# Talking-heads attention with a gated feed-forward on one core: score blocks of 112 rows, two blocks' score products ahead of the first mix, one pool of four PSUM banks

## The chip, the cores and the metric

The kernel runs on one core of a Trainium2 chip. The metric is the device time of one execution in microseconds (us), as the median of several runs. The profile and the trace come from one execution of their own.

## The reference

Attention whose heads are mixed before and after the softmax, then a feed-forward with a gated activation. Batch B = 4, H = 12 heads, S = 448 rows, D = 64; the feed-forward has 768 inputs and 2048 hidden units.

```python
scores = scale * np.matmul(q, k.transpose(0, 1, 3, 2))
scores = np.einsum('bhij,hg->bgij', scores, w_pre)
scores = scores - np.max(scores, axis=-1, keepdims=True)
attn = np.exp(scores)
attn = attn / (np.sum(attn, axis=-1, keepdims=True) + 1e-09)
attn = np.einsum('bhij,hg->bgij', attn, w_post)
x = np.matmul(attn, v)          # then (B, H, S, D) -> (B * S, H * D)
...
h = x @ w_in
g = h * (1.0 / (1.0 + np.exp(-1.702 * h)))
return (g @ w_out).astype(np.float32)
```

## The kernel before

**Scores.** The rows of a batch are cut into four blocks of 120, 120, 120 and 88 rows (`chunk`, `CI`, `NCH`). For each block `b, c` and each of six pairs of heads, `scores` makes two products q k^T of 448 columns, one per head, in two PSUM banks (tiles `qk`, lines 247 and 257). ScalarE (ACT) and VectorE (DVE) copy them to a tile `sc` in SBUF (lines 269 to 279), and `send_scores` (line 283) writes it to a DRAM tensor `sd`, one for each block. Batches 0 and 1 (`b < WHOLE`) work in fp32; batches 2 and 3 carry an upper and a lower fp16 part.

**Steps.** The head mix needs all 12 heads of a row on the partitions. So a step `i` takes 10 rows (`GI`): `gather` (lines 295, 300) reads 120 partitions (10 rows by 12 heads) of 448 values from `sd` into a tile `r`, of which there are four (`AHEAD`), and `mix` multiplies it by a block matrix of `w_pre` into `mx`. A batch has 45 steps (`GPB`, the last with 8 rows), the kernel 180 (`N`). `peak` (DVE) takes the maximum, `expo` (ACT) the exponential and its sum, `shifted` (POOL) and `inverse` (DVE) the reciprocal, `weigh_mix` (POOL) scales the `w_post` matrix to `wr`, and `post_whole` multiplies, with the head mix after the softmax in it, into `pp`; ACT copies that to `p`. In fp16 the names are `weigh`, `upper`, `lower` and `post`. Twelve steps fill one block of `p` (120 rows); `context` then multiplies six pairs of heads by v into `av`, three pairs at a time, and the results become columns of `x`.

**Feed-forward.** A unit is one of 8 slices of the hidden units of one batch: `hidden` (`h`, line 604) and `project` (`po`, line 642), in sessions of 6 matmuls or more. The weights arrive as 64-bit numbers. 16 conversions read them (`w`, three loads of 512 KB each), turn them into fp16 pairs on ACT and DVE and store them in DRAM (`wd`); each unit then loads its two slices (`wt`, 768 KB each). The feed-forward of a batch can start when its last `context` is done.

**PSUM** has eight banks: three of tag `gen` for `qk`, `h` and `po`, one of tag `av`, two for `mx`, two for `pp`.

**What sets the order.** All instructions go out in an order that a planner fixes when the program is built. `add` enters a task with an engine, a planned duration, the tasks it comes after, the buffers it takes and a due time; `run_all` (line 752) picks for each engine the earliest due among the tasks that could start, and books a model of the DMA (`DMA["rate"]`, `lanes` for eight transfers under way). It adds 0.1 us on PE where products of scores or context (`PART`) meet another kind, but doesn't order by it. A task of kind `late` isn't started while more than 1.5 us of transfers are booked; nothing has that kind. All transfers are issued by one queue, SP's, in the planned order.

**The head** is written out by hand (lines 822 to 894): six loads of q and k, 10 products of a matrix of ones, then block 0's six pairs in `gen`, `mx` and `pp` banks by turns, each pair's first 48 rows sent at once (`FRONT`), the four first gathers, the other 72 rows of each pair, and 16 more products of ones (`idle_products(16)`). The planner takes over from there; block 1's pairs come due one by one from step 0 on (`x = pr`), each in a tile of tag `sc`, of which there are three.

## Time and profile before

| | us |
|---|---|
| median of 3 runs | 910.88 (909.64 to 911.83) |
| the profiled execution's own time | 909.49 |
| its span, first to last instruction | 907.8 |
| PE matmul busy in it | 878.1 (97%) |
| DVE, ACT, POOL busy | 633.6, 630.5, 342.8 |

The profiled execution is 1.7 us longer than its span and 1.4 us (0.15%) below the median of the runs. PE is the engine with the least to spare, so the table is read by asking where PE stands idle or is slowed, and who ends that. DMA share is the mean busy share of the core's 16 DMA engines.

### The profile page before, as it was taken

To read this page: it belongs to the slowest core of one execution; us is meant where nothing else is said; L and a number is where in the kernel's file an instruction comes from. 1 tells how busy PE (TensorE), PEld (TensorE's weight loads), DVE (VectorE), ACT (ScalarE), POOL (GpSimd) and SP (SyncE) were. 2 spreads that over 40 slices of the span, in tenths; PEclk is the share of its full clock that TensorE was granted. 3 is DMA by queue.
4 is the path that set the end of the run, shared out by engine and by line. 5 is a ranking of instruction groups with operands and counts; after the bars stand their busy time and mean duration, and the time that the engine had idled before them with its cause. 6 is when DMAs were issued, how large, how long until landed. Compare 5 with 4: busy or idle time off the path is not lost.

```text
span 907.8 us, 19395 instructions
## 1 busy us (share of the span) xinstructions
PE 878.1 (97%) x7062; PEld 538.5 (59%) x7062; DVE 633.6 (70%) x1471; ACT 630.5 (69%) x1391; POOL 342.8 (38%) x538
## 2 busy tenths in 40 slices
PE   7889999999999999999999999999999999999998
PEld 5465666666566566655666656665656666545554
DVE  3668887678789988999678876679676664342233
ACT  2778888698877877876788797676776765323442
POOL 0212222222124221566346745547254663203332
PEclk9989999999999999999999999999999999999999
DMA  7878999998997796688587486568553432243422
GB/s 237 277 285 290 304 326 319 323 308 268 336 331 251 238 300 198 219 234 311 169 265 251 147 258 175 175 180 243 163 154 127 152 97 91 109 139 121 139 74 92
DMA packets 66402, 196.85 MB, mean 217 GB/s; under 512 B 7714, under 2 KB 32546, under 8 KB 66306
## 3 DMA queue, kind: packets, MB, share of 16 engines
q1 hardware_dynamic: 66306, 195.62, 66.7%
q8 instruction: 55, 0.90, 0.4%
q14 instruction: 41, 0.34, 0.1%
HBM read 138.96 MB, written 56.62 MB: 215 GB/s over the span
## 4 chain that ended last, share of the span: by engine, by line
PE 66%; DVE 13%; DMA 7%; ACT 7%; POOL 3%; issue 2%; SPq 1%; ACTq 0%; POOLq 0%; DVEq 0%
PE h L604 19%; PE po L642 18%; PE mx L312 5%; PE pp L363 5%; PE qk L247 3%; PE av L441 3%; PE av L452 3%; DMA vb<-in_v_dram 2%; PE qk L257 2%; DMA sd<-sc 2%; DVE nm L322 2%; DMA r<-sd 2%; PE mx L315 2%; PE pp L400 1%; PE pp L402 1%
## 5 line engine op out<-in xcount | busy, mean ns | idle before, releaser
L604 PE MATMUL h<-x,wt 128*128 128x448 f16 x1152 | 246.5, 352 | 2.0 <-DVE sc L273 0.9
L642 PE MATMUL po<-g,wt 128*128 128x448 f16 x1152 | 239.0, 352 | 2.4 <-DVE th L623 2.1
L604 PEld LDWEIGHTS <-wt 128*128 128x128 f16 x1152 | 108.9, 98 | 105.6 <-issue 15.6
L642 PEld LDWEIGHTS <-wt 128*128 128x128 f16 x1152 | 110.2, 98 | 101.5 <-issue 8.0
L343 POOL TENSOR_SCALAR rs<-sm 120x1 f32<-120x1 f32 x180 | 45.2, 251 | 319.0 <-ACT e L332 311.0
L322 DVE TENSOR_REDUCE nm<-mx 120x1 f32<-120x448 f32 x180 | 111.0, 617 | 36.4 <-PE mx L317 17.9
L670 POOL TENSOR_TENSOR acc<-acc,pt 128x448 f32<-128x448 f32 x69 | 78.7, 1141 | 114.0 <-ACT pt L664 113.3
L363 PEld LDWEIGHTS pp<-wr,e 120*112 120x112 f32 x720 | 85.1, 177 | 37.5 <-issue 18.7
L387 POOL TENSOR_TENSOR a<-w,a 120x448 f16<-120x448 f32 (+1 forms) x90 | 96.0, 1066 | 22.7 <-POOL w L373 11.2
L623 DVE SCALAR_TENSOR_TENSOR th<-th,h 128x448 f32<-128x448 f32 x64 | 39.5, 618 | 92.4 <-ACT th L619 92.1
L363 PE MATMUL pp<-wr,e 120*112 120x120 f32 x720 | 90.9, 270 | 3.9 <-POOL wr L353 3.7
L312 PE MATMUL mx<-r,wa 120*120 120x448 f32 x180 | 87.1, 569 | 5.8 <-DMA r<-sd 4.4
L332 ACT ACTIVATE e<-mx,nm,c 120x448 f32<-120x448 f32 (+1 forms) x90 | 65.3, 725 | 33.2 <-DVE nm L324 23.3
L373 POOL TENSOR_SCALAR w<-e,rs 120x448 f32<-120x448 f32 (+1 forms) x90 | 64.9, 721 | 42.7 <-DVE rs L348 25.1
L666 DVE SCALAR_TENSOR_TENSOR acc<-po,ct,acc 128x448 f32<-128x448 f32 x99 | 66.8, 677 | 15.9 <-PE po L642 15.3
L332 ACT ACTIVATE e<-mx,nm 120x448 f32<-120x448 f32 (+1 forms) x90 | 56.8, 632 | 28.5 <-DVE nm L322 24.9
L664 ACT ACTIVATE pt<-po,ct 128x448 f32<-128x448 f32 x69 | 43.6, 633 | 46.6 <-PE po L642 46.6
L381 ACT ACTIVATE a<-e,rs 120x448 f16<-120x448 f32 (+1 forms) x90 | 59.8, 668 | 20.2 <-DVE rs L348 17.4
L427 DVE TENSOR_TENSOR p<-pp,p 112x480 f16<-112x480 f32 (+1 forms) x90 | 58.3, 649 | 10.8 <-ACT p L423 10.1
L619 ACT ACTIVATE th<-h,ct 128x448 f32<-128x448 f32 x64 | 40.3, 630 | 36.0 <-PE h L604 36.0
L273 DVE SCALAR_TENSOR_TENSOR sc<-qk,sc 120x448 f16<-120x448 f32 (+1 forms) x96 | 55.5, 615 | 10.5 <-ACT sc L269 9.7
L423 ACT CAST p<-pp 112x480 f16<-112x480 f32 (+1 forms) x90 | 50.2, 557 | 17.8 <-PE pp L402 17.6
(141 smaller groups left out, 1604.7 us busy)
## 6 DMA issues: line engine op xcount, KB each, us to landing
...
```

The source lines that it names most:

```text
L312: nc.tensor.matmul(mx[:K, :S], st["wa"][:K, :K], r[:K, :], start=True, stop=True)
L322: nc.vector.tensor_reduce(nm[:K], row["mx", i][:K, :S], axis=AX.X, op=ALU.max, negate=True)
L332: nc.scalar.activation(e[:K], row.pop(("mx", i))[:K, :S], AF.Exp, bias=row.pop(("nm", i))[:K, 0:1], scale=1.0 if b < WHOLE else st["c", b] ...
L363: nc.tensor.matmul(pp[:CP, jc * K:(jc + 1) * K], e[:K, jc * CP:(jc + 1) * CP], wr[:K, :, :n], start=True, stop=True,)
L373: nc.gpsimd.tensor_scalar(w[:K], e[:K], row["rs", i][:K, 0:1], 1.0, op0=ALU.mult, op1=ALU.mult)
L381: nc.scalar.activation(a1[:K], row["e", i][:K], AF.Copy, scale=row["rs", i][:K, 0:1])
L387: nc.gpsimd.tensor_tensor(a2[:K], row.pop(("w", i))[:K], row["a1", i][:K], op=ALU.subtract)
L427: nc.vector.tensor_tensor(p[:, 1], row.pop(("pp", i)), p[:, 0], op=ALU.subtract)
L604: nc.tensor.matmul(h, w[:, i, c, fc * 128:(fc + 1) * 128], x[:, j, c, :], start=(n == 0), stop=(n == len(terms) - 1),)
L642: nc.tensor.matmul(po, w[:, j, fc, e * 128:(e + 1) * 128], g[:, i, fc, :], start=(n == 0), stop=(n == len(terms) - 1),)
L666: nc.vector.scalar_tensor_tensor(a, po, c, a, op0=ALU.mult, op1=ALU.add)
L670: nc.gpsimd.tensor_tensor(a, a, st.pop(("pt", u, e)), op=ALU.add)
```

## The change

The scores are cut into four blocks of 112 rows (`QI`, `block`); steps keep their 10 rows and `p` its 120. So three steps in each batch lie across two blocks and gather in two transfers (`blocks_of`): 12 more gathers in all. In the head the first 64 rows are sent first, not 48, and the 16 products of ones after it are gone. Blocks 1 and 2 of batch 0 (`NEAR`) get tiles of tags that the feed-forward uses later, their products are due at once, and their sends, like the loads of v and of the weights, become `late`, so that gathers go ahead of them. `gen` has four banks, and `context` and the products of ones use it too; tag `av` is gone. Scores come due in twos (`pr % 2`), and PE's pick prefers a product of scores or context by 2 steps of due time when the last one was of these.

```diff
+QI = 112
+    def block(c):
+        return c * QI, QI
...
-    def bank(name, tag="gen", bufs=3):
+    def bank(name, tag="gen", bufs=4):
...
+    def blocks_of(g):
+        i0, n = rows_of(g)
+        return range(i0 // QI, (i0 + n - 1) // QI + 1)
...
+        for c in blocks_of(g):
+            lo, hi = max(i0, c * QI), min(i0 + n, c * QI + QI)
             nc.sync.dma_start(
-                out=t[:n * H], in_=sd[b, c][o:o + n].rearrange("i h t j -> (i h) t j")
+                out=t[(lo - i0) * H:(hi - i0) * H],
+                in_=sd[b, c][lo - c * QI:hi - c * QI].rearrange(form),
             )
...
-            av = bank(f"av_{b}_{c}_{pr}", "av", 1)
+            av = bank(f"av_{b}_{c}_{pr}")
...
-    DMA = {"free": 0.0, "rate": 0.31, "late": 2.2, "issue": 0.4}
+    DMA = {"free": 0.0, "rate": 0.315, "late": 2.2, "issue": 0.4}
...
-                    picks.append(min((x for x in best if x[0] <= t), key=lambda x: (x[2]["due"], x[0]))[1:] + (e,))
+                    picks.append(min((x for x in best if x[0] <= t), key=lambda x: (x[2]["due"] - (2.0 if e == "PE" and last in PART and x[2]["kind"] in PART else 0.0), x[0]))[1:] + (e,))
...
-    FRONT = 48
+    FRONT = 64
...
-    idle_products(16)
...
+    READY, LATER = [19.0, 19.7, 20.4, 21.1], 24.4
...
+    NEAR = {(0, 1, pr): tag for pr, tag in enumerate([("wt0", 2), ("wt1", 2)] * 2 + [("x", 2)] * 2)}
+    NEAR.update({(0, 2, pr): tag for pr, tag in enumerate([("g", 2), ("g", 2), ("acc", 1)] + [("sc", 3)] * 3)})
...
-                gated_by(x) + [inputs.get((n, b, third)) for n in "kq"], x + 0.2, takes=[("gen", h) for h in banks], kind="qk")
+                gated_by(x) + [inputs.get((n, b, third)) for n in "kq"], x + 0.2 + (0.5 * pr + 4 * c - 4) * near, takes=[("gen", h) for h in banks], kind="qk")
...
-        s = add("SP", 0.4, lambda: send_scores(b, c, pr, t["t"]), both, x + 2, size=0.43)
+        s = add("SP", 0.4, lambda: send_scores(b, c, pr, t["t"]), both, x + 2 + (pr + 6 * c - 6) * near, size=0.401, kind="late" if near else "")
...
-                    takes=[("av", av)], kind="av")
+                    takes=[("gen", av)], kind="av")
...
-        return add("SP", 0.4, lambda: load_whole(name, b, i), gated_by(x), x, size=0.459, takes=[(f"{name}p{i}", h)])
+        return add("SP", 0.4, lambda: load_whole(name, b, i), gated_by(x), x, size=0.459, takes=[(f"{name}p{i}", h)], kind="late")
...
-                if b == 0 and c == 1:
-                    x = pr
+                if b == 0 and (c == 1 or (0, c, pr) in NEAR):
+                    x = 0
+                x -= (2 if c else 1) * (pr % 2) * (b > 0 or c > 1)
...
+            if (g + 1) * GI > FRONT and n < GPC:
+                gathers[n]["from"] = LATER
```

The same `late` goes to the staged loads, the weight loads, stores and fetches, and `chunk(b, c)` becomes `block(c)` where scores are made, kept and sent.

**PE after block 0's products.** `qk_c_pr_x` is a product of block c, pair pr; `sums<-ones` the products of ones; `mx<-r` the mix of a step; the last number of a name is a buffer. Before:

```order
L247 MATMUL qk_0_5_1_198<-kf_0_133,qf_0_135 120x448
L835 MATMUL sums<-ones 128x128 x16
L312 MATMUL mx_248<-r_218,wa 120x448
L247 MATMUL qk_1_0_0_250<-kf_0_125,qf_0_127 120x448
L247 MATMUL qk_1_0_1_251<-kf_0_125,qf_0_127 120x448
L312 MATMUL mx_256<-r_220,wa 120x448
L312 MATMUL mx_263<-r_222,wa 120x448
```

Now, from block 1's fourth pair on:

```order
L251 MATMUL qk_1_3_1_251<-kf_0_129,qf_0_131 112x448
L251 MATMUL qk_1_4_0_257<-kf_0_133,qf_0_135 112x448
L251 MATMUL qk_1_4_1_258<-kf_0_133,qf_0_135 112x448
L251 MATMUL qk_1_5_0_264<-kf_0_133,qf_0_135 112x448
L251 MATMUL qk_1_5_1_265<-kf_0_133,qf_0_135 112x448
L321 MATMUL mx_271<-r_218,wa 120x448
L251 MATMUL qk_2_0_0_276<-kf_0_125,qf_0_127 112x448
L251 MATMUL qk_2_0_1_277<-kf_0_125,qf_0_127 112x448
L321 MATMUL mx_284<-r_220,wa 120x448
L251 MATMUL qk_2_1_0_292<-kf_0_125,qf_0_127 112x448
```

All six pairs of block 1 stand ahead of the first mix, without products of ones, and two pairs of block 2 lie among the first mixes.

**SP around the gathers of the twelfth and thirteenth step.** `r<-sd` is a gather, `sd<-sc` a send of scores, `w` a load of weights, `vf` one of v, `wd` a store of converted weights. Before, from the eleventh gather to the thirteenth:

```order
L295 DMA r_437<-sd_0_93 120x448
L283 DMA sd_1_94<-sc_1_4_436 120x896
L295 DMA r_475<-sd_0_93 120x448
L513 DMA w_0_64_0_483<-in_moe_w_out_dram 128x1024
L132 DMA vf_0_497<-in_v_dram 112x1024
L283 DMA sd_1_94<-sc_1_5_501 120x896
L513 DMA w_0_64_1_520<-in_moe_w_out_dram 128x1024
L283 DMA sd_2_95<-sc_2_0_545 120x896
L513 DMA w_0_64_2_584<-in_moe_w_out_dram 128x1024
L579 DMA wd_0_109<-w_0_p 128x3072
L283 DMA sd_2_95<-sc_2_1_573 120x896
L295 DMA r_621<-sd_1_94 120x448
```

Now, from the eleventh to the twelfth, which lies across blocks 0 and 1:

```order
L308 DMA r_424<-sd_0_93 120x448
L522 DMA w_0_64_2_443<-in_moe_w_in_dram 128x1024
L133 DMA vf_0_466<-in_v_dram 112x1024
L287 DMA sd_1_94<-sc_1_3_261 112x896
L287 DMA sd_1_94<-sc_1_4_268 112x896
L133 DMA vf_0_512<-in_v_dram 112x1024
L287 DMA sd_1_94<-sc_1_5_273 112x896
L522 DMA w_0_64_0_545<-in_moe_w_out_dram 128x1024
L287 DMA sd_2_95<-sc_2_0_302 112x896
L133 DMA vf_0_582<-in_v_dram 112x1024
L308 DMA r_593<-sd_0_93 24x448
L308 DMA r_593<-sd_1_94 96x448
```

The twelfth gather now needs block 1, and stands behind nine transfers that were spread over more steps.

**PE in batch 0, where batch 1's scores are made.** Before:

```order
L363 MATMUL pp_1643<-wr_1634,e_1593 112x120 x4
L247 MATMUL qk_0_4_0_1657<-kf_1_1326,qf_1_1334 120x448
L247 MATMUL qk_0_4_1_1658<-kf_1_1326,qf_1_1334 120x448
L312 MATMUL mx_1670<-r_1544,wa 120x448
L363 MATMUL pp_1677<-wr_1665,e_1639 112x120 x4
L247 MATMUL qk_0_5_0_1694<-kf_1_1326,qf_1_1334 120x448
L247 MATMUL qk_0_5_1_1695<-kf_1_1326,qf_1_1334 120x448
L312 MATMUL mx_1703<-r_1577,wa 120x448
L363 MATMUL pp_1713<-wr_1688,e_1667 112x120 x4
```

Now:

```order
L372 MATMUL pp_1553<-wr_1536,e_1512 112x120 x4
L251 MATMUL qk_0_4_0_1567<-kf_1_1370,qf_1_1398 112x448
L251 MATMUL qk_0_4_1_1568<-kf_1_1370,qf_1_1398 112x448
L251 MATMUL qk_0_5_0_1577<-kf_1_1370,qf_1_1398 112x448
L251 MATMUL qk_0_5_1_1578<-kf_1_1370,qf_1_1398 112x448
L372 MATMUL pp_1588<-wr_1558,e_1527 112x120 x4
```

Two pairs follow one another, between post products, where each had its own place between a post product and a mix. Counted over PE's whole order, 116 places where products of scores or context follow another kind become 77.

## Rows read from the trace of the kernel before

**Rows 1.** The page's busy time: engine, us (share of the span), instructions.
```profile
PE 878.1 (97%) x7062; PEld 538.5 (59%) x7062; DVE 633.6 (70%) x1471; ACT 630.5 (69%) x1391; POOL 342.8 (38%) x538
```

**Rows 2.** Stretches: us, busy of each engine (instructions), granted clock, DMA share, GB/s.
```profile
0.00:18.77 18.77, 13.60 (x77) 10.26 (x77) 6.27 (x19) 4.68 (x8) 0.70 (x7) 1.00 0.74 232
18.77:51.05 32.28, 29.00 (x137) 14.93 (x137) 19.05 (x46) 23.49 (x58) 6.04 (x20) 0.95 0.88 285
51.05:67.12 16.07, 12.70 (x122) 10.16 (x120) 10.27 (x26) 10.80 (x28) 1.61 (x4) 0.79 0.74 283
67.12:100.00 32.88, 30.16 (x190) 18.75 (x190) 27.04 (x72) 27.81 (x66) 8.27 (x24) 1.00 0.87 282
100.00:173.30 73.30, 70.32 (x570) 46.84 (x567) 55.66 (x140) 60.57 (x150) 18.93 (x50) 1.00 0.97 324
173.30:249.90 76.60, 76.60 (x492) 47.40 (x490) 61.69 (x160) 66.05 (x163) 16.19 (x41) 1.00 0.94 303
```

**Rows 3.** Timeline of PE: start, us, instruction, [idle before <-releaser]; from the head on.
```profile
10.59 1.77 PE L247 MATMUL qk<-kf,qf 64*120 64x448 f32 x8 [0.49 <-DMA qf<-in_q_dram]
12.29 3.84 PE L835 MATMUL sums<-ones 128*128 128x128 f32 x32
18.77 1.55 PE L312 MATMUL mx<-r,wa 120*120 120x448 f32 x2 [2.64 <-DMA r<-sd]
20.25 1.85 PE L247 MATMUL qk<-kf,qf 64*120 64x448 f32 x4
...
51.05 0.92 PE L312 MATMUL mx<-r,wa 120*120 120x448 f32 x2
...
196.75 0.92 PE L312 MATMUL mx<-r,wa 120*120 120x448 f32 x2
```

**Rows 4.** Idle of PE from 18.77 to 249.9 us by group: busy, mean ns, idle before.
```profile
L363 PE MATMUL pp<-wr,e 120*112 120x120 f32 x544 | 69.3, 271 | 3.9 <-POOL wr L353 3.7
L312 PE MATMUL mx<-r,wa 120*120 120x448 f32 x141 | 68.4, 571 | 5.8 <-DMA r<-sd 4.4 <-ACT w_p L568 0.7 <-ACT e L332 0.7
...
L441 PE MATMUL av<-p,vf 112*64 112x120 f32 (+1 forms) x480 | 27.9, 277 | 3.9 <-ACT p L419 2.6 <-DVE x L475 1.3
```

**Rows 5.** The chain that ended last, from 22 us: start, us, what.
```profile
22.77 4.64 DMA sd<-sc
...
36.12 8.68 DMA r<-sd
```

**Rows 6.** The stretch from 19 to 21 us, columns as in rows 2.
```profile
19.00:21.00 2.00, 2.00 (x4) 0.50 (x5) 0.62 (x1) 0.00 (x0) 0.00 (x0) 0.51 0.72 238
```

**Rows 7.** Timeline of PE in fp32 without waits: a pair of scores among mixes and posts.
```profile
77.67 0.98 PE L363 MATMUL pp<-wr,e 120*112 120x120 f32 x8
78.49 0.92 PE L312 MATMUL mx<-r,wa 120*120 120x448 f32 x2
79.24 0.98 PE L363 MATMUL pp<-wr,e 120*112 120x120 f32 x8
80.15 1.02 PE L247 MATMUL qk<-kf,qf 64*120 64x448 f32 x4
81.10 1.01 PE L312 MATMUL mx<-r,wa 120*120 120x448 f32 x2
81.95 0.98 PE L363 MATMUL pp<-wr,e 120*112 120x120 f32 x8
```

**Rows 8.** Timeline of PE in fp16: a pair of scores between two sessions of the feed-forward.
```profile
432.24 1.30 PE L604 MATMUL h<-x,wt 128*128 128x448 f16 x6
433.47 0.78 PE L257 MATMUL qk<-kp,qp 64*120 64x448 f16 x6
434.18 1.31 PE L604 MATMUL h<-x,wt 128*128 128x448 f16 x6
435.32 0.35 PE L315 MATMUL mx<-r,wm 120*120 120x448 f16 x1
```

**Rows 9.** The page's groups: line, engine, instruction | busy, mean ns | idle before, releaser.
```profile
L604 PE MATMUL h<-x,wt 128*128 128x448 f16 x1152 | 246.5, 352 | 2.0 <-DVE sc L273 0.9
L642 PE MATMUL po<-g,wt 128*128 128x448 f16 x1152 | 239.0, 352 | 2.4 <-DVE th L623 2.1
```

More of the change, by code (lines that the diff above doesn't have):

```diff
@@ L232, in attention_then_feed_forward, with scores @@
             shape, kind = ([H, S], F32) if b < WHOLE else ([H, 2, S], F16)
-            sd[b, c] = dram.tile([chunk(b, c)[1]] + shape, kind, name=f"sd_{b}_{c}", tag=f"sd_{b}_{c}")
-    def bank(name, tag="gen", bufs=3):
+            sd[b, c] = dram.tile([block(c)[1]] + shape, kind, name=f"sd_{b}_{c}", tag=f"sd_{b}_{c}")
+    def bank(name, tag="gen", bufs=4):
         return ps.tile([128, 512], F32, name=name, tag=tag, bufs=bufs)
-    def scores(b, c, pr, tag=("gen", 3)):
-        i0, n = chunk(b, c)
+    def scores(b, c, pr, tag=("gen", 4)):
+        i0, n = block(c)
         two = [bank(f"qk_{b}_{c}_{pr}_{x}", *tag) for x in range(2)]
@@ L830, in attention_then_feed_forward @@
     nc.vector.memset(ones, 1.0)
[L831 removed]
+    last_pp.append(ps.tile([128, 512], F32, name="sums", tag="gen", bufs=4))
     def idle_products(n):
@@ L893, in attention_then_feed_forward @@
         send_scores(0, 0, pr, kept[pr], FRONT)
-    idle_products(16)
-    free.update({"PE": 17.0, "A": 15.0, "D": 16.0, "G": 3.0, "SP": 21.0})
-    DMA["free"] = 22.0
-    lanes.extend([24.0] * 8)
-    held["sc"] = [23.0, 23.5, 24.0]
+    free.update({"PE": 12.7, "A": 13.3, "D": 16.1, "G": 3.0, "SP": 20.5})
+    DMA["free"] = 22.2
+    lanes.extend([19.0, 19.7, 20.4, 21.1, 21.6, 22.2, 22.7, 23.3, 23.8, 24.4])
+    READY, LATER = [19.0, 19.7, 20.4, 21.1], 24.4
+    held["sc"] = [21.6, 22.7, 23.8]
+    held["gen"] = [12.0, 12.9, 13.2, 13.5]
+    held["mx"], held["pp"] = [12.2] * 2, [13.5] * 2
+    held["g"], held["acc"] = [22.2, 23.3], [24.4]
     r_home = {i: [] for i in range(N)}
@@ L975, in product @@
             t["two"] = scores(b, c, pr)
+        near = (b, c, pr) in NEAR
+        home = NEAR.get((b, c, pr), ("sc", 3))
         def place():
-            t["t"] = scores_home(b, c, pr)
+            t["t"] = scores_home(b, c, pr, home)
         j = add("PE", 0.84 if b < WHOLE else 0.61, product,
-                gated_by(x) + [inputs.get((n, b, third)) for n in "kq"], x + 0.2, takes=[("gen", h) for h in banks], kind="qk")
+                gated_by(x) + [inputs.get((n, b, third)) for n in "kq"], x + 0.2 + (0.5 * pr + 4 * c - 4) * near, takes=[("gen", h) for h in banks], kind="qk")
         for n in "kq":
             in_home[n, b, third].append(j)
-        h = add("-", 0.0, place, [j], x + 0.3, 0.0, takes=[("sc", sc)])
+        h = add("-", 0.0, place, [j], x + 0.3, 0.0, takes=[(home[0], sc)])
         both = []
@@ L1038, in whole_load @@
         h = in_home[name, b, i]
-        return add("SP", 0.4, lambda: load_whole(name, b, i), gated_by(x), x, size=0.459, takes=[(f"{name}p{i}", h)])
+        return add("SP", 0.4, lambda: load_whole(name, b, i), gated_by(x), x, size=0.459, takes=[(f"{name}p{i}", h)], kind="late")
     def staged_load(name, b, i, use, x):
         h = []
-        return add("SP", 0.4, lambda: load(name, b, i, use), gated_by(x), x, size=0.459, takes=[("op", h)]), h
+        return add("SP", 0.4, lambda: load(name, b, i, use), gated_by(x), x, size=0.459, takes=[("op", h)], kind="late"), h
     def split_tasks(name, b, x):
@@ L1061, in conversion_tasks @@
             wfs.append(wf)
-            j = add("SP", 0.4, lambda a=a: c["fetch"](a), gated_by(first + 2 * a), first + 2 * a, size=0.524, takes=[("w64", w64)])
+            j = add("SP", 0.4, lambda a=a: c["fetch"](a), gated_by(first + 2 * a), first + 2 * a, size=0.524, takes=[("w64", w64)], kind="late")
             for n, (name, occ) in enumerate((("magnitude", 0.62), ("least", 0.35), ("shift", 0.35), ("rest", 0.61), ("sign", 0.61))):
@@ L1079, in conversion_tasks @@
             pair += [low[a]] + ([u] if a else [])
-        j = conv_done[kind, s] = add("SP", 0.4, c["store"], low, due, size=0.786)
+        j = conv_done[kind, s] = add("SP", 0.4, c["store"], low, due, size=0.786, kind="late")
         pair.append(j)
@@ L1116, in attention_then_feed_forward @@
             n = i + AHEAD
-            gathers[n] = add("SP", 0.4, lambda n=n: gather(n), sends.get((b, g // GPC), []), i,
-                             size=0.215, takes=[("r", r_home[n])], behind=gathers.get(n - 1))
+            gathers[n] = add("SP", 0.4, lambda n=n: gather(n), [j for c in blocks_of(g) for j in sends.get((b, c), [])], i,
+                             size=0.229, takes=[("r", r_home[n])], behind=gathers.get(n - 1))
+            if (g + 1) * GI > FRONT and n < GPC:
+                gathers[n]["from"] = LATER
         step_tasks(i)
@@ L1166, in attention_then_feed_forward @@
                                [conv_done[kind, s]] + gated_by(min(int(due) - 14, N)), due - 6 + 3 * kind,
-                               size=0.786, takes=[(f"wt{kind}", wt_home[kind, u])], behind=got.get((kind, u - 1)))
+                               size=0.786, takes=[(f"wt{kind}", wt_home[kind, u])], kind="late", behind=got.get((kind, u - 1)))
         g_home, lower_g = [], []
```

29 lines of the change are left out of this document (14 added, 15 removed).

## The prediction

> **What bounds the kernel now.** I read the page's busy times first: PE's matmuls fill 878.1 us, 97% of the span, and no other engine reaches 71% [rows 1]. So a change pays only where PE waits, runs at its lower clock, or spends time on the way from one kind of product to another. Next the stretches [rows 2]: PE is idle 5.2, 3.3, 3.4, 2.7 and 3.0 us in the five up to 173.3 us and not at all in the sixth, and its granted clock is 0.95 and 0.79 in the second and third. DMA share is 0.74 to 0.88 up to 100 us and 0.94 to 0.97 from there to 249.9 us. So the first 100 us have slack in both, and after them PE and the transfers are nearly full together; that is the limit to keep in mind. The timeline shows the head [rows 3]: block 0's products end at 12.29 us, the sixteen products of ones do no work of the output, and PE then waits until 18.77 us for the first gather. Of PE's waits from there to 249.9 us, 13.6 us stand before posts (for POOL), mixes (for gathers) and context (for ACT and DVE) [rows 4]; 2.64 us of them are that first wait. The chain says what is late: sends land after 4.64 us at 27.41 us, and only then can the fifth gather go; a gather issued at 36.12 us takes 8.68 us [rows 5]. It waits behind transfers that nothing needs yet.
>
> **The change, part by part.** The sum is made against the profiled execution's 909.5 us.
>
> *Head.* The last first part of a pair is a third larger (64 rows for 48, 57 KB more). At the 238 GB/s of the stretch from 19 us [rows 6] that is 0.24 us; I take 0.4 for its copies and queue, so the first mix starts at 19.2 us. Ahead of it stand six more pairs. Two pairs without a change of kind took 1.70 us (10.59 to 12.29 us, of which 0.95 is a pair's own time among other kinds), so a following pair costs 0.75 [rows 3, 7]; six cost 4.5 us, in time in which PE waited. **Gain 4.5 - 0.4 = 4.1 us.** ACT and DVE copy these twelve products while they, too, have nothing else but DVE's small work on the mix weights; the copies pace the pairs, and the 6.9 us from 12.3 to 19.2 us are the cover. If that cover is short by a pair, 0.75 us goes.
>
> *Products in twos.* From the timeline in fp32 [rows 7]: a post lasts 0.82 us (start to start) before a mix and 0.91 before a pair; a mix 0.75 after a post and 0.85 after a pair; the pair 0.95, against 0.75 for one that follows another. A place saved between two pairs is worth 0.09 + 0.10 + 0.20 = 0.39 us; beside context I count 0.19, without the 0.20. In fp16 [rows 8] a feed-forward session of 1.14 us takes 1.23 before a pair, nothing is added after, and the pair lasts 0.71 against 0.57 for three times the 0.19 us of a matmul: 0.23, and 0.09 beside context. Counted in the order up to the 70th mix (249.9 us before), 47 places become 28: about 14 go between pairs and 5 or 6 beside context, 14 x 0.39 + 6 x 0.19 = **6.6 us**. After it 69 become 49, 6 of them between pairs: 6 x 0.25 + 14 x 0.1 = **2.9 us**. PE is full there, so these count whole.
>
> *Held transfers and the earlier scores.* Of 13.6 us of waits, 11.0 remain behind the first mix. What can come back is bounded by nothing (other waits of the same size) and 11.0 us. The fifth and sixth gather no longer wait for the second parts of block 0, and fewer large transfers stand among the gathers of steps 5 to 11. Against that stands SP's order: the twelfth gather stands behind nine transfers, and needs block 1's sends among them. So I follow the transfers. Counted from the shapes in SP's order, 13.9 MB are issued by the twelfth gather (12.6 before). By 51.05 us, when the twelfth mix ran, the kernel before had moved 18.77 us at 232 GB/s and 32.28 us at 285, 13.6 MB [rows 2, 3]; the change keeps the DMA busier from 20 to 28 us, so I put the twelfth mix at 50 us. There PE has done four pairs and a post more than before (4 x 0.75 + 0.82 = 3.8 us), a lead of nearly 5 us. From the twelfth gather to the 58th the change issues 37.8 MB. From 51.05 to 196.75 us, the 58th mix before, the stretches' rates average 307 GB/s [rows 2, 3]; at that rate it takes 123 us, to 173 us. Since the weights come later, the feed-forward starts after 58 mixes instead of 50, and PE is behind by 42 of its matmuls and two posts less two pairs: 7 x 1.14 + 1.6 - 1.5 = 8.1 us. So the lead is 196.75 - 173 - 8.1 = **about 15 us** at the 58th mix. That holds the head's gain, most of the pairs' and the waits. PE alone would allow 4.1 + 6.6 + 11.0 = 21.7 us, and with no wait recovered 10.7 us; I take 15, what the transfers allow.
>
> *Four common banks.* h and po waited 2.0 and 2.4 us in all [rows 9]. A fourth bank can take from 0 to 4.4 us; context now takes one of the four, which could add as much again, since context waited 3.9 us for its own bank's copies [rows 4]. I take 1 us, near the middle of the two.
>
> *Costs.* Twelve more gathers are some 0.4 us each on SP, beside 8.68 us that a gather may take anyway [rows 5]: nothing on the path while SP has room. ACT, DVE and POOL get the same instructions as before, with 448 columns each.
>
> Sum: 15 + 2.9 + 1 = 18.9 us less, 890.6 us for this execution; the runs' median stands 1.4 us above it, so I forecast **891 us** with rounding.
>
> *The skill on the transfers.* The Trainium skill ("DMA: Bandwidth & Descriptors", section on why a DMA increments its semaphore by 16) says that a transfer runs on the largest number up to 16 of DMA engines that divides the slowest dimension of both sides. By that a send of 112 rows uses 16 engines, where 120 rows use 15 and 88 rows 11. No row here shows a transfer engine by engine. By the page an estimate would be 1/16 less on some 14 MB of sends between the twelfth and the 58th mix, 3 us, and a forecast of 888 us.
>
> **The rivals.**
>
> *A. Transfers take more of it back.* From the twelfth to the 58th mix they run at the 283 GB/s of the stretch from 51.05 to 67.12 us [rows 2] because PE asks for gathers and sends faster than the queue mixes in the held ones. Then 133.6 us pass, the lead is 196.75 - 50 - 133.6 - 8.1 = 5 us, and with 2.9 + 1 after it the time is 901 us. For it: DMA share is 0.97 already at 324 GB/s. Against: 324 and 303 GB/s were reached just there.
>
> *B. Slower: the held transfers starve PE.* The rate falls because the gathers stand in SP's one queue behind loads and sends, each waiting for its own release, and DMA stands idle meanwhile, while the feed-forward, which fills PE's gaps from 173.3 us on, starts eight mixes later. It decides below 265 GB/s: 37.8 MB then take 142.6 us, the lead is -4, and the 3.9 us after it are used up. At 250 GB/s (151.2 us) the time is 918 us. For it: the first 18.77 us made only 232 GB/s, and a 4.64 us landing held the queue once [rows 2, 5]. Against: no longer stretch after that fell under 282.
>
> *C. The clock.* The granted clock was 1.00 up to 18.77 us, with products of ones until 16.1 us, and 0.51, the 1.2 GHz level, from 19 to 21 us, after 2.64 us of idle [rows 2, 3, 6]. If it falls while the pairs wait for copies, a pair takes 1.85 us instead of 0.95 [rows 3, 7], six cost 5.4 us more, the first mix is at about 22 us and 3 us of the head are gone: 894 us. The Trainium skill ("TensorE: Matmul & The Clock Gate", part 1) says that the half rate is the default and activity releases it, which would speak against taking out products that only keep PE busy. The row agrees in that the clock fell after the idle wait, not during the products; but now pairs stand in that wait, so I hold this for unlikely.
>
> *D. It doesn't count.* The places saved could be filled by waits of the same length, the lead lost by the feed-forward's later start: within 1.8 us of before. The full PE from 173.3 us on speaks against it.
>
> **How the numbers follow.** Forecast 0.60, A 0.15, C 0.08, D 0.03, B 0.11; 0.03 for more than 30 us. The forecast's own range goes from all that PE allows (21.7 + 2.9 + 4.4, 29 us less than 909.5, 880.5, so 881 to 882 as a median) to no wait recovered (10.7 + 2.9, 896, so 897). With A and C in it the range is 881 to 904 us; left out are B, D, and what is better still. Faster by over 0.2%, about what a measurement of this kernel can tell from no change: 0.60 + 0.15 + 0.08 + 0.03 = 0.86; slower 0.11; the same 0.03.
>
> **What would show it.** Right: the first mix near 19.2 us after six more pairs; the twelfth mix near 50 us, the 58th near 173 us and the first h just behind it; the 70th mix about 15 us earlier than 249.9; sessions of two pairs lasting 1.70 us in fp32 and well under 1.42 in fp16; PE's waits up to there under 8 us. Wrong: DMA share below 0.9 between 60 and 170 us with PE waiting for r (B); share full at a rate of 285 GB/s (A); a clock of 0.5 between 12 and 19 us (C); new waits for gen banks at h or po beyond 4.4 us.

## The result and the profile after

The changed kernel takes 899.38 us as the median of four runs (897.95 to 904.53); the kernel before, beside it, 910.26 (909.51 to 911.83). The ratio is 0.9888 [0.9846, 0.9931]: 10.9 us less, where 19 to 20 were forecast. The profiled execution took 898.76 us, its span 896.7.

The stretches of the changed kernel, cut as in [rows 2]: us, busy of PE, PEld, DVE, ACT and POOL (instructions), granted clock, DMA share, GB/s.

```profile
0.00:18.77 18.77, 15.50 (x68) 9.24 (x68) 8.57 (x23) 8.54 (x16) 0.70 (x7) 1.00 0.76 242
18.77:51.05 32.28, 28.56 (x136) 17.09 (x136) 17.31 (x44) 22.37 (x58) 6.50 (x22) 0.88 0.98 299
51.05:67.12 16.07, 13.40 (x54) 7.32 (x54) 10.73 (x29) 11.40 (x28) 3.36 (x11) 0.71 0.89 268
67.12:100.00 32.88, 31.39 (x270) 21.84 (x270) 27.23 (x74) 29.91 (x73) 8.92 (x23) 1.00 0.94 318
100.00:173.30 73.30, 70.71 (x580) 47.78 (x575) 57.94 (x151) 64.57 (x161) 17.76 (x51) 1.00 0.96 313
```

The second stretch, where the kernel before had slack, now has a DMA share of 0.98, and PE's clock in it is lower than before, not higher (0.88 for 0.95). The third is no better than before: PE busy for 13.40 of 16.07 us at a clock of 0.71.

PE's timeline, columns as in [rows 3]: the head, a session of two pairs, and the border between blocks 0 and 1.

```profile
10.36 7.38 PE L251 MATMUL qk<-kf,qf 64*112 64x448 f32 x32 [0.52 <-DMA qf<-in_q_dram]
19.26 1.69 PE L321 MATMUL mx<-r,wa 120*120 120x448 f32 x2 [1.52 <-DMA r<-sd]
...
35.20 1.76 PE L251 MATMUL qk<-kf,qf 64*112 64x448 f32 x8
36.89 1.01 PE L321 MATMUL mx<-r,wa 120*120 120x448 f32 x2
...
42.84 0.92 PE L321 MATMUL mx<-r,wa 120*120 120x448 f32 x2
43.83 1.04 PE L372 MATMUL pp<-wr,e 120*112 120x120 f32 x8
46.92 1.94 PE L372 MATMUL pp<-wr,e 120*112 120x120 f32 x8 [2.05 <-POOL wr L362]
48.66 0.44 PE L112 MATMUL pp<-w_m,ones 128*128 128x3 f32 x2
48.95 1.92 PE L372 MATMUL pp<-wr,e 120*112 120x120 f32 x8
53.16 1.82 PE L321 MATMUL mx<-r,wa 120*120 120x448 f32 x2 [2.28 <-DMA r<-sd]
```

The first mix starts at 19.26 us. Two pairs last 1.69 us from start to start (35.20 to 36.89). The row at 42.84 is the eleventh mix, that at 53.16 the twelfth. Between them PE has three posts and one small product, no scores: 2.05 us of waiting for POOL, then products at 1.9 us for 0.98, then 2.28 us of waiting for the gather. The 58th mix is a row at 179.25 us and the first session of h comes behind it:

```profile
179.25 0.92 PE L321 MATMUL mx<-r,wa 120*120 120x448 f32 x2
...
180.83 1.30 PE L613 MATMUL h<-x,wt 128*128 128x448 f16 x6
```

SP's timeline around the twelfth gather (start, us, what, how many), in two stretches, so that its two parts stand apart:

```profile
34.85 0.39 SPq L522 DMA_DIRECT2D w<-in_moe_w_in_dram  x1
35.29 0.42 SPq L133 DMA_DIRECT2D vf<-in_v_dram  x1
36.06 0.78 SPq L287 DMA_DIRECT2D sd<-sc  x2
37.38 0.32 SPq L133 DMA_DIRECT2D vf<-in_v_dram  x1
37.98 0.39 SPq L287 DMA_DIRECT2D sd<-sc  x1
...
43.75 0.29 SPq L308 DMA_DIRECT2D r<-sd  x1
...
47.67 1.68 SPq L308 DMA_DIRECT2D r<-sd  x4
```

What SP waited for from 43 to 54 us (us in total, times, longest), and how long the send of 37.98 us took:

```profile
SPq L308 <- DMA sd<-sc: 3.6, 1, 3.6
...
DMA to landing us min/median/max: 9.6/9.6/9.6
```

The last send of block 1 goes out at 37.98 us, behind three loads and two sends of the 3.2 us before it, and lands 9.6 us later. The twelfth gather's part that reads block 0 is issued at 43.75 us. Then SP waits 3.6 us for that send to land, and issues the part that reads block 1 at 47.67 us, with three later gathers behind it. The twelfth mix starts 5.5 us after that.

PE's idle time by group, columns as in [rows 4]: first for 18.77 to 249.9 us, then, for the small products of line 112 (with a matrix of ones they add up squares over the partitions, from which v, k and the weights get their scales), from 249.9 to 556 us; last the page's groups that answer to [rows 9].

```profile
L372 PE MATMUL pp<-wr,e 120*112 120x120 f32 x560 | 72.7, 274 | 5.9 <-POOL wr L362 5.0 <-ACT p L428 0.8
L321 PE MATMUL mx<-r,wa 120*120 120x448 f32 x144 | 71.6, 582 | 5.3 <-DMA r<-sd 4.7 <-ACT e L341 0.5
L450 PE MATMUL av<-p,vf 112*64 112x120 f32 (+1 forms) x480 | 25.3, 263 | 0.0
...
L112 PE MATMUL pp<-w_m,ones 128*128 128x3 f32 x12 | 2.1, 242 | 3.4 <-ACT p L428 1.5 <-DVE p L436 1.3 <-ACT waste L100 0.6
L112 PE MATMUL pp<-mk,ones 128*128 128x6 f32 x2 | 0.4, 264 | 1.5 <-DVE p L436 1.5
```

```profile
L613 PE MATMUL h<-x,wt 128*128 128x448 f16 x1152 | 246.0, 353 | 1.9 <-DMA wt<-wd 1.1
L651 PE MATMUL po<-g,wt 128*128 128x448 f16 x1152 | 240.0, 352 | 0.6 <-DVE acc L675 0.4
```

The 13.6 us of [rows 4] have become 11.2: context's 3.9 are gone, the posts' 3.9 have become 5.9. h and po wait 2.5 us for 4.4. The last two rows of the first fence are 4.9 us of waits before line 112; in the kernel before, all such small products (its line 111) waited 1.4 us in that stretch.

**One measure for all kernels.** PE's *delay* at a step is the time of that step's row maximum on DVE, less the work that stands ahead of its mix in PE's order, at full speed and without waits, from the durations of [rows 3, 7, 8] (0.75 us a mix, 0.82 a post, 0.75 a pair in a row, 1.14 six matmuls of the feed-forward), with some 5 us for a block's context and 0.07 for a small product. At the end it is the span less 824.9 us, the same sum for the whole kernel. It holds waits, lower clock, changes of kind and a late DVE together, and shows where two kernels part even when the feed-forward starts at other steps. Each row comes from one profiled execution, which can lie some us from its kernel's median (no_twos took 907.25 us for a median of 903.46, no_head 893.87 for 896.73).

| kernel | step 1 | 11 | 12 | 13 | 25 | 58 | 70 | end |
|---|---|---|---|---|---|---|---|---|
| before | 15.9 | 25.5 | 25.3 | 33.0 | 40.4 | 51.0 | 53.5 | 82.9 |
| the change | 12.0 | 17.3 | 25.3 | 26.3 | 31.6 | 41.4 | 44.5 | 71.8 |
| no_twos | 11.4 | 17.2 | 25.0 | 26.0 | 31.3 | 43.8 | 46.4 | 80.6 |
| no_head | 15.9 | 20.3 | 20.8 | 22.7 | 30.9 | 42.9 | 45.8 | 67.2 |
| sends_first | 11.4 | 19.9 | 24.0 | 23.8 | 36.3 | 45.6 | 48.4 | 73.5 |
| pairs_at_border | 12.6 | 16.0 | 25.4 | 26.4 | 32.0 | 42.1 | 45.3 | 72.0 |
| rows_only | 15.5 | 24.4 | 32.8 | 35.2 | 40.1 | 54.1 | 58.2 | 90.7 |
| twos_only | 15.6 | 25.5 | 25.0 | 31.7 | 36.1 | 51.7 | 55.3 | 87.0 |
| no_hold | 12.0 | 21.2 | 30.3 | 31.0 | 38.0 | 53.5 | 56.1 | 82.6 |
| banks_3_1 | 13.5 | 19.4 | 22.7 | 25.2 | 29.8 | 41.7 | 44.6 | 78.3 |
| head_block_1 | 11.2 | 20.5 | 20.5 | 20.8 | 35.0 | 42.4 | 44.5 | 72.6 |
| head_block_1_held | 11.4 | 18.5 | 31.4 | 32.2 | 36.4 | 44.7 | 46.7 | 73.2 |
| no_head_no_ones | 16.3 | 21.0 | 22.5 | 23.4 | 31.7 | 44.5 | 47.4 | 70.2 |
| no_head_no_hold | 15.8 | 23.0 | 28.9 | 29.0 | 34.7 | 44.1 | 46.5 | 73.5 |

The first two rows give the reading that the experiments then try. The change is 3.9 us ahead at the first step, 8.2 at the eleventh, level at the twelfth, 6.7 ahead at the thirteenth (the kernel before pays its border one step later), 9.0 at the 70th, and 11.1 at the end.

### The profile page after: what moved, and what is told of

Same layout as the page of the kernel before. It is cut to its first block, busy times and chain, and to the rows that moved or that the text cites. A ratio compares the mean times of both kernels' runs of the same rounds, so it can differ in the third digit from the quotient of the medians.

```text
span 896.7 us, 19356 instructions
## 1 busy us (share of the span) xinstructions
PE 870.7 (97%) x7030; PEld 538.3 (60%) x7030; DVE 627.1 (70%) x1476; ACT 626.1 (70%) x1385; POOL 340.7 (38%) x534
## 5 line engine op out<-in xcount | busy, mean ns | idle before, releaser
L331 DVE TENSOR_REDUCE nm<-mx 120x1 f32<-120x448 f32 x180 | 110.7, 617 | 36.4 <-PE mx L321 19.2
L679 POOL TENSOR_TENSOR acc<-acc,pt 128x448 f32<-128x448 f32 x64 | 74.9, 1171 | 106.6 <-ACT pt L673 105.7
L396 POOL TENSOR_TENSOR a<-w,a 120x448 f16<-120x448 f32 (+1 forms) x90 | 98.4, 1094 | 32.2 <-issue 14.2
L675 DVE SCALAR_TENSOR_TENSOR acc<-po,ct,acc 128x448 f32<-128x448 f32 x104 | 70.0, 677 | 16.7 <-PE po L651 16.4
L341 ACT ACTIVATE e<-mx,nm 120x448 f32<-120x448 f32 (+1 forms) x90 | 57.1, 634 | 23.8 <-DVE nm L331 16.3
L390 ACT ACTIVATE a<-e,rs 120x448 f16<-120x448 f32 (+1 forms) x90 | 59.8, 665 | 15.4 <-DVE rs L357 13.2
L673 ACT ACTIVATE pt<-po,ct 128x448 f32<-128x448 f32 x64 | 40.5, 632 | 42.9 <-PE po L651 42.9
L362 POOL TENSOR_SCALAR wr<-wp,rs 120x120 f32<-120x120 f32 (+1 forms) x90 | 44.5, 495 | 58.3 <-DVE rs L357 41.1
L277 DVE SCALAR_TENSOR_TENSOR sc<-qk,sc 112x448 f16<-112x448 f32 x96 | 55.3, 616 | 12.5 <-ACT sc L273 12.1
```

The source lines that it names most:

```text
L331: nc.vector.tensor_reduce(nm[:K], row["mx", i][:K, :S], axis=AX.X, op=ALU.max, negate=True)
L341: nc.scalar.activation(e[:K], row.pop(("mx", i))[:K, :S], AF.Exp, bias=row.pop(("nm", i))[:K, 0:1], scale=1.0 if b < WHOLE else st["c", b] ...
L390: nc.scalar.activation(a1[:K], row["e", i][:K], AF.Copy, scale=row["rs", i][:K, 0:1])
L396: nc.gpsimd.tensor_tensor(a2[:K], row.pop(("w", i))[:K], row["a1", i][:K], op=ALU.subtract)
L675: nc.vector.scalar_tensor_tensor(a, po, c, a, op0=ALU.mult, op1=ALU.add)
L679: nc.gpsimd.tensor_tensor(a, a, st.pop(("pt", u, e)), op=ALU.add)
```

## The experiments

All times stand against the kernel before, timed beside them on the same chip (910.18, 909.5 and 908.89 us in the three groups of four). Where nothing else is said, an edit is made to the changed kernel. That kernel was not timed again beside them: its ratio comes from its own four runs, so a difference from it is safe only where the two intervals don't overlap.

### Is the lead that of the pairs, or of the head? (no_twos, no_head)

```diff
-    ... x[2]["due"] - (2.0 if e == "PE" and last in PART and x[2]["kind"] in PART else 0.0) ...
+    ... x[2]["due"] ...
-                x -= (2 if c else 1) * (pr % 2) * (b > 0 or c > 1)
```

> The change without its two rules that put products of scores and context together (108 places instead of 77, 40 instead of 28 up to the 70th mix). Theory 1, PE sets the pace: the 31 places come back at 0.1 to 0.39 us each, about 4 us up to the 70th mix and 3 us after it, so 906 us. Theory 2, the transfers set the pace up to the 70th mix: nothing is lost up to there, about 3 us after it, so 902 us, and the 70th mix is where the change has it (within 1 us).

Measured: 903.46 us, ratio 0.9930 [0.9906, 0.9954], so by the medians the twos are worth 4.1 us; the interval still overlaps the change's [0.9846, 0.9931], so that they are worth anything is likely but not settled. PE's order has 108 places where scores or context follow another kind for 77, and 40 for 28 up to the 70th mix. The table puts 1.9 us of the loss ahead of the 70th step and 6.9 behind it, the other way round than predicted (6.6 and 2.9). The profiled execution of no_twos lies 3.8 us above its median, so the 6.9 is the less certain of the two. Ahead of the 70th step the saved places weren't filled by waits: up to there PE waits 13.5 us in the change and 14.7 in no_twos. The change has the lower granted clock (0.97 for 0.98 over the first 249.9 us), which may be part of it.

```diff
+    idle_products(16)
...
-    NEAR = {(0, 1, pr): tag ...}
-    NEAR.update({(0, 2, pr): tag ...})
+    NEAR = {}
...
-                if b == 0 and (c == 1 or (0, c, pr) in NEAR):
-                    x = 0
+                if b == 0 and c == 1:
+                    x = pr
```

(and the planner's own start for PE goes with the products of ones, from 12.7 to 17.0 us).

> The change with its head undone: block 1's and block 2's pairs in the planner's turn as before, their sends not held, the sixteen products of ones back. Theory 1: the 4 us of the head are lost, 903 to 904 us, the twelfth mix a few us later than 53. Theory 2: the head's lead is lost at the border of blocks 0 and 1 anyway, so 899 to 900 us, with the 30th mix where the change has it.

Measured: 896.73 us (893.87 to 899.75), ratio 0.9876 [0.9847, 0.9906], below what both theories gave. Without the early pairs of blocks 1 and 2 the kernel is not slower than the change (0.9888 [0.9846, 0.9931]); the intervals overlap, and the head's 4.1 us don't appear. The table says where they went: no_head starts 3.9 us later, level with the kernel before, and is 4.5 us *ahead* at the twelfth step. Its timeline of PE at the border:

```profile
44.43 1.76 PE L251 MATMUL qk<-kf,qf 64*112 64x448 f32 x8
46.12 2.05 PE L372 MATMUL pp<-wr,e 120*112 120x120 f32 x16
48.01 0.29 PE L112 MATMUL pp<-w_m,ones 128*128 128x3 f32 x2
48.16 0.99 PE L321 MATMUL mx<-r,wa 120*120 120x448 f32 x2
```

Where the change waits, no_head has two pairs of block 2 and two posts to do. The twelfth mix (48.16) finds its rows there: block 1's last send goes out no earlier than in the change (38.39 us), but lands sooner, and SP issues the gather's second part at 43.49 us after 0.6 us of waiting for it. The clock stays at its full level (the stretch from 51.05 to 67.12 us has 1.00, PE busy 14.65).

### Can the border be mended? (sends_first, pairs_at_border)

```diff
-    ... send_scores(b, c, pr, t["t"]), both, x + 2 + (pr + 6 * c - 6) * near, ...
+    ... send_scores(b, c, pr, t["t"]), both, x + 2 + (pr + 6 * c - 6) * near - (6 + 0.5 * pr) * (near and c == 1), ...
```

> The change with block 1's sends due ahead of the loads of v and of the weights in SP's queue. Theory 1 (the twelfth gather stands behind nine transfers, so PE empties and its clock falls): the twelfth mix comes at 47 to 50 us instead of 53, without the half-speed stretch from 47 to 59 us, and 4 to 6 us are gained, 894 us. Theory 2 (transfers set the pace): the twelfth mix is earlier, but the 58th within 1.5 us of the change's, and the time 898 to 900 us.

Measured: 899.04 us, 0.9892 [0.9868, 0.9917]. Block 1's sends go ahead of the loads of v and weights, SP no longer waits for one of them, and the twelfth mix starts at 49.19 us, after 1.26 us of waiting for its gather. Others follow: PE waits 0.92, 1.35, 1.21 and 2.32 us up to 60 us, and the delay at the 25th step is 4.7 us more than the change's. Theory 2 had the time right, but not the path: at the 58th step the delay is 4.2 us above the change's, not level with it.

```diff
-    ... x + 0.2 + (0.5 * pr + 4 * c - 4) * near, takes=[("gen", h) for h in banks], kind="qk")
+    ... x + 0.2 + (0.5 * pr + 4 * c - 4 + 5 * (c == 2)) * near, takes=[("gen", h) for h in banks], kind="qk")
```

> The change with the last three pairs of block 2 due later, so that they lie between the eleventh and the twelfth mix, where PE waits; SP's queue is nearly as in the change. Theory 1: 2.5 us of PE's 4.6 us of waits there are filled with work that stands later otherwise, and PE's clock falls later or for less time: 2 to 5 us gained, 895 to 897 us. Theory 2: within 1 us of the change, since the twelfth gather lands no earlier.

Measured: 898.8 us, 0.9893 [0.9871, 0.9914]. Two of block 2's pairs now run at 43.12 us, and the twelfth mix still starts at 54.43 us, after a wait of 3.98 us for its gather. SP, in turn, waits 5.2 us for block 1's last send before it issues that gather. Work for PE at the border doesn't move the twelfth mix, since it waits for its transfer.

### The parts alone (rows_only, twos_only, no_hold, banks_3_1)

rows_only is the kernel before with the rows of the change and nothing else: `QI`, `block`, `blocks_of` and the gathers of the diff above, with the planner's sizes and due times that belong to them. twos_only is the kernel before with the two lines that no_twos takes out.

```diff
+QI = 112
+    def block(c):
+        return c * QI, QI
+    def blocks_of(g):
...
+        for c in blocks_of(g):
```

> The kernel before with one part of the change alone: blocks of 112 rows, with gathers over two blocks (110 places where products of scores or context follow another kind, against 116). Theory 3, the places saved on PE make most of the gain: 908 to 910 us. Theory 4, fewer and better timed transfers make it: 903 to 906 us.

> The kernel before with the two rules that put products of scores and context together, and nothing else (98 places against 116). Theory 3: 18 places at 0.1 to 0.39 us, 3 to 6 us less, 904 to 907 us. Theory 4: within 1.5 us of 910.

Measured: rows_only 917.52 us, 1.0067 [1.0034, 1.0099]; twos_only 912.38 us, 1.0037 [1.0014, 1.0061]. Both are slower than before, which none of the theories had. rows_only needs block 1 one step earlier, and pays at the border: its delay grows by 8.4 us at the twelfth step, and PE waits 5.04 us there.

```profile
54.37 1.10 PE L251 MATMUL qk<-kf,qf 64*112 64x448 f32 x4
60.51 1.82 PE L321 MATMUL mx<-r,wa 120*120 120x448 f32 x2 [5.04 <-DMA r<-sd]
```

```diff
-    ... x + 2 + (pr + 6 * c - 6) * near, size=0.401, kind="late" if near else "")
+    ... x + 2 + (pr + 6 * c - 6) * near, size=0.401)
...
-    ... load_whole(name, b, i), gated_by(x), x, size=0.459, takes=[(f"{name}p{i}", h)], kind="late")
+    ... load_whole(name, b, i), gated_by(x), x, size=0.459, takes=[(f"{name}p{i}", h)])
```

and the same for the staged loads, weight loads, stores and fetches.

> The change without held transfers: sends of blocks 1 and 2 and the loads of v and weights go out by their due times alone. 77 places as in the change; the feed-forward starts after 50 mixes, not 58. Theory 3: 898 to 901 us. Theory 4: gathers wait behind loads again, the lead at the 25th mix is gone, 904 to 908 us.

Measured: 907.53 us, 0.9976 [0.9955, 0.9998]. So in this kernel the held transfers are worth 8.2 us, the largest of the parts tried, and the two intervals are apart. Without them the stretch over the border reads:

```profile
51.05:67.12 16.07, 7.98 (x24) 4.87 (x25) 9.08 (x24) 8.82 (x22) 1.71 (x6) 0.62 0.95 336
```

The transfers run at 336 GB/s, for 268 in the change, and PE is busy half of it: what is moved is not what PE waits for. By the twelfth maximum at 61.3 us 17.4 MB had been moved (283 GB/s from 0), in the change by 56.2 us 15.4 MB (274 GB/s).

```diff
-    def bank(name, tag="gen", bufs=4):
+    def bank(name, tag="gen", bufs=3):
...
-            av = bank(f"av_{b}_{c}_{pr}")
+            av = bank(f"av_{b}_{c}_{pr}", "av", 1)
...
-                    takes=[("gen", av)], kind="av")
+                    takes=[("av", av)], kind="av")
```

> The change with its PSUM banks as before (three common ones and one for context). The two rules find fewer places to join: 95 against 77. Theory 3: 18 places come back, 3 to 6 us, 902 to 905 us, with the loss growing evenly through the steps. Theory 4: 898 to 901 us.

Measured: 905.1 us, 0.9950 [0.9926, 0.9974]: four common banks are worth 5.7 us in this kernel, not 1 (the intervals overlap by 0.0005). Up to the 70th step the two kernels have the same delay (44.6 and 44.5), from there on banks_3_1 loses 6.4 us more. Its groups of h and po:

```profile
L613 PE MATMUL h<-x,wt 128*128 128x448 f16 x1152 | 245.9, 352 | 2.7 <-ACT pt L673 1.3
L651 PE MATMUL po<-g,wt 128*128 128x448 f16 x1152 | 241.5, 354 | 3.7 <-DVE th L632 2.1
```

They wait 6.4 us in place of 2.5: 3.9 us more. The rest may be the 18 places that this kernel has more (95 for 77), which no run takes by themselves.

### Can the head's lead be kept? (head_block_1, head_block_1_held)

```diff
-    NEAR.update({(0, 2, pr): tag for pr, tag in enumerate([("g", 2), ("g", 2), ("acc", 1)] + [("sc", 3)] * 3)})
...
-    ... x + 2 + (pr + 6 * c - 6) * near, size=0.401, kind="late" if near else "")
+    ... x + 2 + pr * near, size=0.401)
```

head_block_1_held has the first of these edits alone.

> Of the head only block 1's six pairs are kept, their sends neither held nor behind the loads; block 2's pairs stand again between the mixes where the planner puts them. T7 (the head's 4 us are lost because TensorE has no products left between the 11th and the 13th mix): first mix near 19 us as in the change, the 12th and 13th mix follow without a wait of over 2.5 us together as in no_head, so no_head's 896.7 less about 3 to 4: 892 to 894. T8 (the moment of the 12th mix is set by the transfers of block 1, whatever TensorE has to do): the lead is lost at the 12th mix again, 896 to 899.

> The same, but block 1's sends stay held and due as in the change, behind the loads. T7: 892 to 895, if block 2's pairs are work enough to cover the wait for the later sends. T8: the 12th mix comes as late as in the change, near 56 us, and the time is 897 to 900. Against head_block_1 the difference is what holding those sends is worth in itself.

Measured: 900.99 us, 0.9908 [0.9883, 0.9934], and 900.2 us, 0.9916 [0.9883, 0.9949]. In head_block_1 T7's mechanism came true and its time didn't: the delay hardly grows from the eleventh step to the thirteenth (20.5 to 20.8), so the border can be crossed with block 1 done in the head. But the delay then grows by 14.2 us to the 25th step, where the change's grows by 5.3, and not by waits for transfers; at the 70th step the two kernels are level. PE's timeline there, and then DVE's:

```profile
82.47 1.01 PE L321 MATMUL mx<-r,wa 120*120 120x448 f32 x2 [0.19 <-ACT e L341]
...
93.25 1.85 PE L321 MATMUL mx<-r,wa 120*120 120x448 f32 x2 [4.45 <-ACT e L341]
```

```profile
89.29 0.41 DVE L533 TENSOR_SCALAR w_f<-w_f 128x512 f32<-128x512 f32 x1
89.62 0.68 DVE L543 SCALAR_TENSOR_TENSOR w_f<-w,w_f 128x512 int32<-128x512 int32 x1
...
91.16 0.68 DVE L543 SCALAR_TENSOR_TENSOR w_f<-w,w_f 128x512 int32<-128x512 int32 x1
91.76 0.61 DVE L331 TENSOR_REDUCE nm<-mx 120x1 f32<-120x448 f32 x1
```

The mix of 82.47 us gets its maximum only at 91.76: The conversions of weights (`w_f`), whose loads were moved behind block 1's sends, now stand ahead of it in DVE's order, without a gap. Both `mx` banks stay taken so long, and PE stands idle from 88.8 to 93.25 us; the mix after it runs at half speed (1.85 us). The timeline of waits names ACT's exponential, but DVE is what it waits for.

With the sends behind the loads, in head_block_1_held, the loss comes at the twelfth step, all at once. PE's timeline, and one row of ACT's:

```profile
48.95 0.38 PE L112 MATMUL pp<-w_m,ones 128*128 128x3 f32 x2
58.24 0.59 PE L112 MATMUL pp<-mv,ones 112*128 112x6 f32 x2 [8.91 <-ACT waste L100]
59.12 5.12 PE L321 MATMUL mx<-r,wa 120*120 120x448 f32 x6 [0.29 <-DMA r<-sd]
```

```profile
56.71 0.63 ACT L100 ACTIVATE waste<-vf 112x512 bf16<-112x512 f32 x1 [1.51 <-DMA vf<-in_v_dram]
```

PE's next instruction is a small product for the scale of v, which needs the last load of v; the twelfth mix stands behind it, and its gather lands no earlier (0.29 us more of waiting). That gather, too, is issued late: SP waits 4.9 us for DVE's copy of a later pair, whose send stands ahead, and reaches the gather's two parts at 50.51 and 52.6 us. The edits of the two kernels differ only in when block 1's sends are due, and the twelfth maximum is at 48.2 us in one (12.9 MB moved, at 269 GB/s from 0) and at 61.0 in the other (17.1 MB at 281). At the 25th step their delays are only 1.4 us apart, at the 70th 2.2. What the sends gain at one border the loads, put back by them, cost at the next.

### The products of ones, and holding without the head (no_head_no_ones, no_head_no_hold)

```diff
-    idle_products(16)
```

(from no_head), and for the other the edit of no_hold on no_head.

> no_head without the 16 products of ones. T9 (TensorE must be at work just before the first mix to be granted full speed there, rival C of the prediction): the first mixes run at half speed, 898.5 to 901 and a granted clock near 0.5 at 19 to 22 us. T10 (the products of ones do nothing for the clock that the rest of the head doesn't do): within 1 us of no_head, 895.7 to 897.7.

> no_head without the rule that holds loads and sends until a gather is on its way. T11 (the rule's 8 us come from the loads that would otherwise run beside the gathers, whatever the head does): 903.5 to 906.5, with the first half of the loss before 70 us. T12 (the rule pays for the head's held sends alone, which no_head doesn't have): 896 to 899.

Measured: 895.91 us (894.46 to 898.29), 0.9857 [0.9834, 0.9879], by its median the fastest kernel of the study; and 899.14 us, 0.9885 [0.9866, 0.9904]. Without the ones PE idles 6.82 us before the first mix, and the stretches behind it read, without and then with them:

```profile
19.00:21.00 2.00, 1.27 (x2) 0.80 (x3) 0.00 (x0) 0.00 (x0) 0.00 (x0) 0.50 0.93 195
21.00:24.00 3.00, 3.00 (x5) 0.80 (x3) 1.55 (x3) 1.50 (x4) 0.19 (x1) 0.50 0.94 281
24.00:28.00 4.00, 4.00 (x23) 2.13 (x22) 2.40 (x8) 2.69 (x7) 1.49 (x5) 1.00 0.90 203
```

```profile
19.00:21.00 2.00, 1.68 (x3) 0.86 (x4) 0.00 (x0) 0.00 (x0) 0.00 (x0) 0.50 0.88 220
...
21.00:24.00 3.00, 3.00 (x5) 0.74 (x3) 1.85 (x4) 1.93 (x5) 0.20 (x2) 0.50 0.97 277
24.00:28.00 4.00, 4.00 (x19) 2.06 (x19) 2.02 (x5) 2.04 (x6) 1.47 (x5) 0.79 0.83 177
```

The clock is at half either way; PE waits 2.49 us after the ones as well. T10 holds, and rival C's worry for the products of ones falls. Holding is worth at most 2.4 us without the head (899.14 less 896.73, across two groups; 0.8 us by the ratios, whose intervals overlap) and 8.2 with it: mostly it mends what the head does to the queue. T12 is the nearer.

no_head_no_ones stands at 0.9857 [0.9834, 0.9879] and the change at 0.9888 [0.9846, 0.9931]: the simpler kernel is at least as fast. Whether it is faster the intervals don't settle; no run of the two beside each other was made.

## Why the prediction was right and wrong

Right: faster, and within the range. The first mix came at 19.26 us (19.2 predicted), pairs in a row at 1.69 us for two (1.70). That the range held is partly luck. The forecast's own range ended at 897 us, and 899.38 is in the stated one only because A and C widened it; A's 901 us lies nearer than the 891, though its mechanism, a lower rate, didn't come. The 891 itself is a slip: 890.6 and 1.4 make 892. From the twelfth step to the 58th the working from bytes nearly held: 37.8 MB in 123 us were predicted, 38.7 MB in 124.3 were measured between the two maxima (56.2 and 180.5 us; 15.4 and 54.1 MB moved by then, from the rate of the stretch up to each). D, B and A fell: PE's gain shows, and the transfers ran at 318, 313 and 310 GB/s.

**The step that failed is "the lead is 196.75 - 173 - 8.1 = about 15 us at the 58th mix".** (The terms give 15.65.) The 58th mix came at 179.25 us, so the lead is 196.75 - 179.25 - 8.1 = 9.4 us (9.6 in the table). Half of the miss is the sentence before it, "I put the twelfth mix at 50 us"; the other half is the stretch behind it, 126.1 us from mix to mix for 123. I took 13.9 MB issued ahead of the twelfth gather and let the mix start when these had been moved. The bytes were right: by 50 us 14.0 MB had been moved (279 GB/s from 0). But the mix started at 53.16 us, because it didn't need the bytes, it needed one transfer: block 1's last send, issued at 37.98 us, landed 9.6 us later, and the gather's second part went out only then, at 47.67 us. And I took it that PE had a lead to keep there. It had 8.2 us at the eleventh step, and gave all of it back before the twelfth, since all pairs of blocks 1 and 2 had been done by then and nothing else was due. The experiments bear this out: with block 1's sends landed in time and pairs left for the border (no_head, head_block_1), PE crosses it for at most 2.4 us from the eleventh step to the thirteenth; with pairs left but the gather's second part issued at 48.85 or 52.6 us (pairs_at_border, head_block_1_held) it waits 3.98 and 8.9 us in one piece. What remains is that the loads of v and the weights have to come at some time: sends_first and head_block_1 lose at the next steps what they gain at this one.

By the sum "PE alone would allow 4.1 + 6.6 + 11.0", the waits failed most: 1.3 us of the 11.0 behind the first mix came back (9.7 remain, 11.2 less 1.52). All of PE's waits up to there were to be under 8 us and are 11.3.

*The head* was right as a number at the first mix (3.9 us) and wrong as a gain in the end: no_head is 2.6 us faster by its median, within the interval. A wait was filled with work that was then missing at the next wait. no_head also shows a gain that the sum left out: it is 5.2 us ahead of the kernel before at the eleventh step with its first mix no earlier, and no_head_no_hold is still 2.5 ahead there. Beside the held transfers and the fourth bank these steps are touched by the larger first part (64 rows for 48) and the planner's settings for the DMA, which no run takes alone.

*The clock.* Rival C looked for a fall while the pairs ran; that didn't come (1.00 up to 18.77 us). The fall came where PE ran dry: between 46.92 and 59.5 us products take 1.8 to 1.9 us for 0.9 to 1.0. One less the clock, times the stretch, is 0.12 x 32.28 + 0.29 x 16.07 = 8.5 us, against 0.05 x 32.28 + 0.21 x 16.07 = 5.0 before [rows 2], an upper estimate, since PE also waits in these stretches. These 3.5 us had no term. The Trainium skill ("TensorE: Matmul & The Clock Gate", part 1) calls the half rate the default, which activity lifts; the rows agree, in that each fall read here follows a wait of PE.

*Products in twos* were 4.1 us by the medians, not 9.5, and by the two profiles mostly after the 70th step. *Four common banks* were 5.7 us within the change, not 1: 3.9 of them are waits of h and po, inside my 0 to 4.4, and the rest lies outside what I counted. Against the kernel before, h and po got back 1.9 us. A likely reason why the banks count for more within the change, not shown, is that [rows 9] are of a kernel whose three banks didn't have to serve products in twos. At these values, less the 1.9 us that no_twos loses ahead of the 70th step, the two would give some 8 us behind it, and the change's lead grew by only 2.1 there (9.0 to 11.1; 3.9 predicted). Part of what was lost is in sight: 4.9 us of waits before small products stand after 249.9 us, for 1.4 before, two of them 1.5 us long, and after one of these, at 461.94 us, the clock fell (0.91 from 460 to 480 us, 1.8 us). Another part may be the rows of 112, which alone made the kernel before 6 us slower.

So the parts don't add: rows alone +6.1 us and twos alone +3.4 against the kernel before (ratio less one, times 910), while twos, holding and banks are worth 4.1, 8.2 and 5.7 us within the change, and the head nothing that shows. That the head needs the loads to be held is shown (no_hold against no_head_no_hold). That the rows need the sends to land early and the twos the fourth bank is only likely: rows_only waits 5.04 us for the gather that its rows move a step ahead, and twos_only has three banks, but no run leaves the rows out of the change or gives twos_only the fourth bank. What stays open, too, is how much of the 21 to 34 us that the kernels lose after the 70th step belongs to an edit itself and how much to the new order that the planner finds with it; the change, no_head and no_hold all have 77 places, and lose 27.3, 21.4 and 26.5 us there (no_head in an execution 2.9 us below its median).

The Trainium skill's rule ("DMA: Bandwidth & Descriptors", why a DMA increments its semaphore by 16), by which sends of 112 rows would use 16 engines where 120 use 15, gave an estimate of 3 us less. rows_only, which has these sends, and 12 more gathers, shows no higher rate: 286, 286 and 262 GB/s in the three stretches from 18.77 to 100 us, for 285, 283 and 282 [rows 2]. No row here shows single engines, so the rule stands untried, but no gain of that size is seen.
